# The second half of a block's first output products one step later, with a filter load and a transposed class moved

## The chip, the cores and the metric

The kernel runs on one core of a Trainium2 chip. The time is device microseconds of one execution. A core has TensorE (PE, matrix products into the banks of PSUM), VectorE (DVE), ScalarE (ACT), GpSimd (POOL) and SyncE (SP), each with its own queue of instructions that it works through in order, and 16 DMA engines that the queues share.[...]

## The reference

Two layers, on 8 sequences of 3008 tokens with 256 channels. The first multiplies each sequence's spectrum by a complex filter; the second is a feed-forward layer with a swish whose slope is given per hidden unit.

```
X = rfft(x, axis=1);  Y = X * (filt_r + 1j*filt_i);  y = irfft(Y, n=3008, axis=1)
h = y.reshape(24064, 256) @ w_in          # 256 -> 2048
g = h * sigmoid(beta * h)
out = g @ w_out                           # 2048 -> 256, float32
```

## The kernel before

The feed-forward layer is the backbone. Its 24064 tokens are 47 blocks of 512, and a block has 16 steps, one for each 128 hidden units (`fb`, 0 to 15): 752 steps. A step (the loop at L812) first makes the hidden layer, two products of 512 columns into a PSUM tile `hps` (L825), from a pool of two banks. ScalarE then makes the activation tile `gT` from it (L834; a ring of four). Then come the units that the plan has for this step. Last come the output products of the step two earlier (`LAG = 2`): four products of 256 columns, one for each 128 tokens of the block (`tb`), with `gT` as the loaded weights and a row group of `wout_sb` as the moving operand (L860). They add up over the 16 steps of a block into two accumulators `acc`, each one PSUM bank that holds two `tb`. The accumulators come from the pool `opsum`, which has three banks. After `fb` 15 each accumulator is copied to an `ost` tile and stored by SyncE. VectorE does these copies, except that ScalarE does the first of the two in the blocks 0 to 5.

The transform is done as products in stages, 3008 = 47 x 64. For sequence 0 it is done ahead of the loop, without a trip to DRAM, and its last stage is in four classes (`g`, 0 to 3), each of which makes 752 columns of the transformed sequence that the blocks then read in order. Class 0 is made before the loop. The others are units in the plan: `turn_z(g, i)` transposes (eight products on TensorE into the tile `pz`, L536, and a copy on VectorE), twice for a class, and `last_z(g, i)` makes four small products and a copy (L544), four times for a class. A block of sequence 0 can run only when its classes are there.

For the sequences 1 to 7 the stages are units in the plan. `s1` (16 for a sequence; L619) makes one product and a copy into a buffer `a1`, and each fourth one issues a store to DRAM on SyncE (L624). `a1` comes from the pool `apool` of three, in which the first class of sequence 0 also has its place. `a2_read` reads that back in four DMAs (L631). `s23` (15 for a sequence) does two products (L641), three VectorE operations with the filter tiles `frr` and `fri` (L652, L653, L656), a sum on GpSimd (L657), and three units later two more products (L667) and a copy on ScalarE. `zz_read` and `s4` (L544) give the outputs. All PSUM tiles of these units come from `fpsum`, three banks.

The plan is a table from step to units. `place(a, z, units, clear, per)` (L696) spreads units evenly over the steps a to z, in order; a step that already holds `per` units is passed over. Units run in a step in the order in which they were placed.

The tile `frr` has two uses. Ahead of the loop two thirds of it (columns 8 to 23) stage `w_out` on its way in; then it takes the real part of the filter, in three parts of 1 MB, each four DMAs of 256 KB on SyncE (`load_filter`, L127). In the kernel before, the first part is issued ahead of the loop (L520), behind a marker DMA (L506) that waits for x of sequence 1 to land. The other two parts are issued in step 15 (`uf`, L731), behind `a2_read(1)`.

Of the kernel before, what the change touches and what calls it, by code (L numbers as in the profile page):

```python
# [9 lines left out]
P = 128  # L10
# [14 lines left out]
M = 64  # L25
H = M // 2
NK = 24
J = 32
KG = 6
NG = NK // KG  # L30
JG = 8
# [6 lines left out]
def kernel(  # L38
# [10 lines left out]
    nc = tc.nc  # L49
# [8 lines left out]
    NFB = FF // P  # L58
# [29 lines left out]
    frr = consts.tile([P, NK, D], F32, name="frr", tag="frr")  # L88
# [12 lines left out]
    wout_sb = wpool.tile([P, NFB, D], BF16, name="wout_sb", tag="wout_sb")  # L101
# [25 lines left out]
    def load_filter(f_sb, filt, at, k0, n, eng):  # L127
        lo = AP(filt.tensor, filt.offset + k0 * D, [[N1 * D, H], [1, n * D]])
        hi = AP(filt.tensor, filt.offset + (N1 - k0) * D, [[N1 * D, H], [-D, n], [1, D]])
        return [  # L130
            lambda: eng.dma_start(
                f_sb[at : at + H, k0 : k0 + n, :].rearrange("p k d -> p (k d)"), lo
            ),
            lambda: eng.dma_start(f_sb[at + H : at + M, k0 : k0 + n, :], hi),
        ]
# [13 lines left out]
    def scale_wout(i):  # L149
        fs = slice(i * WG, (i + 1) * WG)  # L150
        nc.gpsimd.tensor_tensor(
            wout_sb[:, fs, :],
            staged(i),
            rbeta_sb[:, fs].unsqueeze(2).broadcast_to([P, WG, D]),
            ALU.mult,
        )
# [360 lines left out]

    for i in range(4):
        scale_wout(i)
    for at in (0, M):  # L520
        for go in load_filter(frr, filt_r, at, 0, JG, nc.sync):
            go()

    ys = {}
    ys[0] = ypool.tile([P, NDC, NK * P], BF16, name="y", tag="y")
# [4 lines left out]
    def turn_z(g, i, on_act=False):  # L530
        if g not in zz0:
            zz0[g] = zzpool.tile([KP, JG, D], BF16, name="zz", tag="zz")
        pz = fpsum.tile([P, 4, D], BF16, name="pz", tag="f")
        for e in range(4):
            for dc in range(NDC):
                nc.tensor.transpose(  # L536
                    pz[:KP, e, dc * P : (dc + 1) * P], z_t[:, dc, JG * g + 4 * i + e, :], ident[:]
                )
        evac(zz0[g][:, 4 * i : 4 * i + 4, :], pz[:KP], on_act)
# [24 lines left out]
    def last_z(g, i, on_act, own=None):  # L564
        jq, dc = divmod(i, NDC)
        c = g * JG // JC + jq
        yv = ys[0][:, dc, c * CLS : (c + 1) * CLS].rearrange("p (n j) -> p n j", j=JC)

        n0 = NP if jq == 0 else (TB - CLS) // JC
        return last4(zz0[g], t4b, JC * jq, dc, yv, on_act, own, n0)  # L570
# [55 lines left out]
    def a2_read(b):  # L626
        s = st[b]
        s["a2"] = []
        for h in range(NG):
            t = a2pool.tile([P, KG, D], BF16, name="a2", tag="a2")  # L630
            nc.sync.dma_start(t[:], s["d1c"][:, h * KG : (h + 1) * KG, :])  # L631
            s["a2"].append(t)
# [41 lines left out]
    def zz_read(b):  # L674
        s = st[b]
        s["zz"] = []
        for h in range(NJG):
            t = zzpool.tile([KP, JG, D], BF16, name="zz", tag="zz")
            nc.sync.dma_start(t[:], s["d2r"][:, h * JG : (h + 1) * JG, :])
            s["zz"].append(t)  # L680
# [15 lines left out]
    def place(a, z, units, clear=False, per=1):  # L696
        last_at = a
        for n, go in enumerate(units):
            at = a + (z - a) * n / max(1, len(units) - 1)
            at = max(int(at), last_at)  # L700
            if clear and (at % NFB < 2 or at % NFB > 13):
                at += (2 - at) % NFB
            while len(plan.get(at, ())) >= per:
                at += 1
            plan.setdefault(at, []).append(go)
            last_at = at
        return last_at

    def u1(b, act=False):
        def unit(i):  # L710
            def go():
                if i == 0:
                    start(b)
                s1(b, i, act and i % 2 == 1)

            return go

        return [unit(i) for i in range(J // 2)]

    def u23(b):  # L720
        return [lambda i=i: s23(b, i) for i in range(NK // 2 + VLAG)]

    def u4(b, act=False):
        return [lambda i=i: s4(b, i, act and i % 2 == 1) for i in range(J // 2)]

    def uz(g, act=False):
        return [lambda i=i: turn_z(g, i) for i in range(2)] + [
            lambda i=i: last_z(g, i, act) for i in range(2 * NDC)
        ]

    def uf():  # L731
        return [
            go
            for k0 in range(JG, NK, JG)
            for at in (0, M)
            for go in load_filter(frr, filt_r, at, k0, JG, nc.sync)
        ]


    def ut(n):  # L740
        return [
            lambda k=k: nc.vector.tensor_scalar_mul(
                t3[M:P, k : k + NK // n], t3b[M:P, k : k + NK // n], -1.0
            )
            for k in range(0, NK, NK // n)
        ]
# [6 lines left out]

    place(2, 14, uz(1, True))
    place(15, 29, uz(2))
    place(34, 58, uz(3, True))

    first_step = [(S * b // TB) * NFB for b in range(B + 1)]
    if B > 1:
        units = u1(1, True)  # L760
        place(3, 8, units[: J // 4], per=2)
        at = place(9, 14, units[J // 4 :], per=2)
        place(at + 1, at + 1, [lambda: a2_read(1)] + uf(), per=9)
        place(14, 20, ut(4), per=2)
        at = place(25, 56, u23(1), per=2)
        assert at < 60
        place(60, 60, [lambda: zz_read(1)], per=9)
        place(67, 79, u4(1), per=2)
    if B > 2:
        place(36, 36, ux(2), per=9)  # L770
        at = place(50, 66, u1(2, True), per=3)
        assert at < 74
        place(74, 74, [lambda: a2_read(2)], per=9)
    for b in range(2, B):
        a = first_step[b - 1]
# [36 lines left out]
    for s in range(len(steps) + LAG):  # L812
        if s < len(steps):
            i, fb = steps[s]
            t0 = i * TB
            tn = min(TB, TOK - t0)
            hps = hpsum.tile([P, TB], F32, name="hps", tag="hps")
            pos = t0
            while pos < t0 + tn:
                b, n0 = divmod(pos, S)  # L820
                ln = min(S - n0, t0 + tn - pos)
                if s == 0:
                    ln = min(ln, CLS - n0 % CLS)
                for dc in range(NDC):
                    nc.tensor.matmul(  # L825
                        hps[:, pos - t0 : pos - t0 + ln],
                        lhsT=win_sb[:, dc, fb * P : (fb + 1) * P],
                        rhs=ys[b][:, dc, n0 : n0 + ln],
                        start=(dc == 0),
                        stop=(dc == NDC - 1),  # L830
                    )
                pos += ln
            gT = gpool.tile([P, TB], BF16, name="gT", tag="gT")
            nc.scalar.activation(  # L834
                gT[:, :tn], hps[:, :tn], ACT.Silu, scale=beta_sb[:, fb : fb + 1]
            )
            blk[s] = gT
        if s in plan:
            for go in plan[s]:
                go()  # L840
        if s >= LAG:
            i, fb = steps[s - LAG]
            t0 = i * TB
            tn = min(TB, TOK - t0)
            nch = tn // P
            gT = blk.pop(s - LAG)

            last = i == NBLK - 1
            if fb == 0 and not last:
                acc = [opsum.tile([P, 2, D], F32, name="acc", tag="acc") for _ in range(2)]  # L850
            elif fb == 0:
                acc = [
                    (fpsum if h % 2 else opsum).tile(
                        [P, 1, D], F32, name="acc", tag="f" if h % 2 else "acc"
                    )
                    for h in range(nch)
                ]
            per = acc[0].shape[1]
            for tb in range(nch):
                nc.tensor.matmul(  # L860
                    acc[tb // per][:, tb % per, :],
                    lhsT=gT[:, tb * P : (tb + 1) * P],
                    rhs=wout_sb[:, fb, :],
                    start=(fb == 0 and tb % per == 0),
                    stop=(fb == NFB - 1),
                    skip_group_check=True,
                )
            if fb == NFB - 1:
                for h, a in enumerate(acc):
                    if h * per % 2 == 0:  # L870
                        ost = ostp.tile([P, 2, D], F32, name="ost", tag="ost")
                    c = h * per % 2
                    on_act = h == 0 and i < 6 or last and h % 2 == 0
                    evac(ost[:, c : c + per, :], a[:], on_act)
                    eng = nc.scalar if last and h >= 2 else nc.sync
                    store(t0 + h * per * P, per * P, ost[:, c : c + per, :], eng)
# [30 lines left out]
```

## Time and profile before

| | |
|---|---|
| median of 3 runs | 789.7 us (789.14 to 792.92) |
| profiled execution | 789.54 us |
| its span, first to last instruction | 787.6 us |
| TensorE busy | 776.5 us, 99% |
| ScalarE busy | 597.0 us, 76% |
| VectorE busy | 393.6 us, 50% |
| GpSimd busy | 144.5 us, 18% |
| granted TensorE clock | 1.000 |
| DMA | 91.46 MB, 116 GB/s on average |

A line of a group of instructions has the line of the kernel, engine, operation, output and inputs, shape and count; then the busy time in us and the mean of one in ns; then the idle time of the engine just before them and what ended most of it. A line of a timeline has start and duration in us, engine, line, operation, tiles and count, and in brackets idle time before it with its releaser. The chain is the work that ended last, followed back from the last instruction.

### The profile page before, as it was taken

What the parts mean: (1) busy time and instruction counts of PE and PEld (TensorE: products, weight loads), DVE (VectorE), ACT (ScalarE), POOL (GpSimd) and SP (SyncE); (2) the same over time, 40 slices, a digit from 0 to 9 for tenths busy, and PEclk for the clock granted to TensorE, in tenths of its full rate; (3) what the DMA queues carried; (4) which work ended last, traced back from release to release, by engine and by line L of the source; (5) the groups of instructions that cost most, each with busy time, mean ns of one, the idle gap of its engine ahead of it and who ended that gap; (6) DMA issues with size and microseconds to landing.
All of it is one profiled execution on the core that took longest, in us unless ns stands there. A gap on an engine that the chain in (4) does not pass through costs nothing.

```text
span 787.6 us, 15550 instructions
## 1 busy us (share of the span) xinstructions
PE 776.5 (99%) x6111; PEld 548.0 (70%) x6111; DVE 393.6 (50%) x645; ACT 597.0 (76%) x922; POOL 144.5 (18%) x143
## 2 busy tenths in 40 slices
PE   8999999999999999999999999999999999999998
PEld 5767667766777667876668766686667766776665
DVE  8837835646436564465635746267462761500101
ACT  6977886886678866788677876778767788677776
POOL 8512500420014200231002310024000340000000
PEclk9999999999999999999999999999999999999999
DMA  9978673517801187012850238412370214100101
GB/s 192 251 170 226 161 202 134 126 67 198 223 27 67 51 211 206 28 67 96 202 170 27 95 105 185 151 56 84 111 208 28 75 67 127 48 34 28 55 27 54
DMA packets 84185, 91.46 MB, mean 116 GB/s; under 512 B 4498, under 2 KB 74276, under 8 KB 83154
## 3 DMA queue, kind: packets, MB, share of 16 engines
q1 hardware_dynamic: 81008, 73.95, 30.5%
q0 software_dynamic: 2816, 16.26, 10.6%
q8 instruction: 48, 0.79, 0.4%
q14 instruction: 25, 0.20, 0.1%
q10 hardware_dynamic: 288, 0.26, 0.1%
HBM read 57.16 MB, written 46.66 MB: 132 GB/s over the span
## 4 chain that ended last, share of the span: by engine, by line
PE 93%; DVE 4%; issue 2%; DMA 1%; ACT 1%; DVEq 0%; ACTq 0%
PE acc L860 41%; PE hps L825 40%; PE ps L619 3%; PE ps L544 3%; PE ps L641 2%; PE ps L667 2%; PE pw L187 1%; DVE ost L109 1%; DMA d<-a 1%; DVE qb_t L444 1%; DVE pb_t L444 0%; DVE q_t L656 0%; ACT gT L834 0%; DVE q_t L653 0%; PE psa L325 0%
## 5 line engine op out<-in xcount | busy, mean ns | idle before, releaser
L834 ACT ACTIVATE gT<-hps,beta_sb 128x512 bf16<-128x512 f32 x752 | 516.2, 687 | 175.3 <-PE hps L825 164.1
L860 PE MATMUL acc<-wout_sb,gT 128*128 128x256 bf16 x3008 | 455.2, 272 | 1.2 <-ACT ost L107 0.2
L825 PE MATMUL hps<-y,win_sb 128*128 128x512 bf16 (+8 forms) x1730 | 447.7, 351 | 0.3 <-ACT gT L834 0.3
L860 PEld LDWEIGHTS <-gT 128*128 128x128 bf16 x3008 | 285.4, 98 | 132.4 <-issue 4.3
L825 PEld LDWEIGHTS <-win_sb 128*128 128x128 bf16 x1730 | 164.9, 98 | 24.8 <-issue 0.6
L657 POOL TENSOR_TENSOR v_t<-p_t,q_t 128x512 bf16<-128x512 f32 x84 | 106.7, 1271 | 393.1 <-DVE q_t L656 390.2
L109 DVE COPY ost<-acc 128x512 f32<-128x512 f32 (+1 forms) x88 | 56.3, 678 | 193.8 <-PE acc L860 190.6
L109 DVE CAST a<-ps 96x512 bf16<-96x512 f32 x96 | 65.8, 686 | 90.0 <-PE ps L619 85.3
L111 DVE TENSOR_SCALAR y<-ps 128x376 bf16<-128x376 f32 (+1 forms) x119 | 64.5, 545 | 62.6 <-PE ps L544 62.4
L652 DVE TENSOR_TENSOR p_t<-ps,frr 128x512 f32<-128x512 f32 x84 | 58.1, 692 | 32.0 <-PE ps L641 27.9
L656 DVE TENSOR_TENSOR q_t<-ps,fri 64x512 f32<-64x512 f32 x84 | 58.3, 694 | 1.2
L653 DVE SCALAR_TENSOR_TENSOR q_t<-ps,fri 64x512 f32<-64x512 f32 x84 | 57.4, 684 | 1.1
L544 PEld LDWEIGHTS <-zz 96*128 96x128 bf16 x512 | 35.3, 97 | 30.6 <-issue 1.9
L107 ACT ACTIVATE z<-ps 128x512 bf16<-128x512 f32 x84 | 49.5, 590 | 1.0 <-PE ps L667 0.9
L619 PE MATMUL ps<-xg,t 94*96 94x512 bf16 x112 | 42.0, 381 | 0.0
L544 PE MATMUL ps<-t,zz 96*128 96x94 bf16 x448 | 36.7, 204 | 0.0
L667 PE MATMUL ps<-v_t,t 128*128 128x256 bf16 x168 | 32.1, 273 | 0.8 <-DVE q_t L656 0.8
L641 PE MATMUL ps<-a,t 128*128 128x256 bf16 x168 | 32.1, 273 | 0.0
L118 POOL DMA_DIRECT2D xg<-in_x_dram x22 | 12.1, 552 | 101.7 <-PE acc L860 97.7
L641 PEld LDWEIGHTS <-t 128*128 128x128 bf16 x168 | 15.8, 98 | 14.6
L619 PEld LDWEIGHTS <-t 94*96 94x96 bf16 x112 | 13.8, 123 | 12.1
L667 PEld LDWEIGHTS <-t 128*128 128x128 bf16 x168 | 15.4, 98 | 8.5 <-DVE q_t L656 1.5
(120 smaller groups left out, 196.3 us busy)
## 6 DMA issues: line engine op xcount, KB each, us to landing
out_dram<-ost SPq DMA_DIRECT2D x80, 256.0 KB, 2.1
d<-a SPq DMA_DIRECT2D x28, 384.0 KB, 3.8
a<-d SPq DMA_DIRECT2D x28, 384.0 KB, 4.9
d<-z SPq DMA_DIRECT2D x28, 384.0 KB, 2.3
zz<-d SPq DMA_DIRECT2D x28, 384.0 KB, 6.7
xg<-in_x_dram POOLq DMA_DIRECT2D x6, 1280.0 KB, 10.1
frr<-in_filt_r_dram SPq DMA_DIRECT2D x12, 256.0 KB, 7.7
out_dram<-ost SPq DMA_DIRECT2D x18, 128.0 KB, 2.1
```

Source lines behind the costliest of these rows:

```text
L109: nc.vector.tensor_copy(dst, src)
L111: nc.vector.tensor_scalar_mul(dst, src, scale)
L544: nc.tensor.matmul(ps[:, e, :NP], lhsT=zz[:, jj + e, dc * P : (dc + 1) * P], rhs=tab[:], start=True, stop=True,)
L619: nc.tensor.matmul(ps[:KP], lhsT=t1[:], rhs=s["x"][:, 2 * i : 2 * i + 2, :], start=True, stop=True)
L641: nc.tensor.matmul(ps[:, e, :], lhsT=t2[:, k0 + e, 3:5, :].rearrange("p c k -> p (c k)"), rhs=s["a2"][g][:, kk + e, :], start=True, stop=True,
L652: nc.vector.tensor_tensor(p_t[:], ps[:], frr[:, ks_, :], ALU.mult)
L656: nc.vector.tensor_tensor(q_t[:M], ps[M:P], fri[M:P, ks_, :], ALU.mult)
L657: nc.gpsimd.tensor_tensor(v_t[:], p_t[:], q_t[:], ALU.add)
L667: nc.tensor.matmul(ps[:, e, :], lhsT=t3[:, k0 + e, :], rhs=v_t[:, e, :], start=True, stop=True)
L825: nc.tensor.matmul(hps[:, pos - t0 : pos - t0 + ln], lhsT=win_sb[:, dc, fb * P : (fb + 1) * P], rhs=ys[b][:, dc, n0 : n0 + ln], start=(dc ...
L834: nc.scalar.activation(gT[:, :tn], hps[:, :tn], ACT.Silu, scale=beta_sb[:, fb : fb + 1])
L860: nc.tensor.matmul(acc[tb // per][:, tb % per, :], lhsT=gT[:, tb * P : (tb + 1) * P], rhs=wout_sb[:, fb, :], start=(fb == 0 and tb % per = ...
```

## The change

There are three edits.

In the loop, the output products of `fb` 0 are cut in two. The step makes those of the first accumulator only. Those of the second are made in the following step, between the two pairs of `fb` 1.

The first third of the filter load is taken from ahead of the loop and put in the plan at step 10, ahead of that step's other units. `uf` gets bounds for it. For the first stage of sequence 1 the limit of units in a step is raised from 2 to 9, so that the entry at step 10 pushes none of them away.

The units of class 3 of sequence 0 are placed in two pieces: the two `turn_z` at the steps 20 to 24, and the four `last_z` spread over 34 to 58. Before, the six were spread over 34 to 58.

```
-    for at in (0, M):
-        for go in load_filter(frr, filt_r, at, 0, JG, nc.sync):
-            go()
...
-    def uf():
+    def uf(a, z):
         return [
             go
-            for k0 in range(JG, NK, JG)
+            for k0 in range(a, z, JG)
             for at in (0, M)
             for go in load_filter(frr, filt_r, at, k0, JG, nc.sync)
         ]
...
-    place(34, 58, uz(3, True))
+    units = uz(3, True)
+    place(20, 24, units[:2], per=2)
+    place(34, 58, units[2:])
...
-        at = place(9, 14, units[J // 4 :], per=2)
-        place(at + 1, at + 1, [lambda: a2_read(1)] + uf(), per=9)
+        place(10, 10, uf(0, JG), per=9)
+        at = place(9, 14, units[J // 4 :], per=9)
+        place(at + 1, at + 1, [lambda: a2_read(1)] + uf(JG, NK), per=9)
...
-            for tb in range(nch):
+            todo = [(gT, fb, tb) for tb in range(nch)]
+            if fb == 0:
+                todo, late = todo[: nch // 2], todo[nch // 2 :]
+            elif fb == 1:
+                todo[nch // 2 : nch // 2] = late
+            for g_, f_, tb in todo:
                 nc.tensor.matmul(
                     acc[tb // per][:, tb % per, :],
-                    lhsT=gT[:, tb * P : (tb + 1) * P],
-                    rhs=wout_sb[:, fb, :],
-                    start=(fb == 0 and tb % per == 0),
-                    stop=(fb == NFB - 1),
+                    lhsT=g_[:, tb * P : (tb + 1) * P],
+                    rhs=wout_sb[:, f_, :],
+                    start=(f_ == 0 and tb % per == 0),
+                    stop=(f_ == NFB - 1),
                     skip_group_check=True,
                 )
```

By the plan the units move so:

| unit | step before | step after |
|---|---|---|
| `turn_z(3, 0)`, `turn_z(3, 1)` | 34, 38 | 20, 24 |
| `last_z(3, 0)` to `last_z(3, 3)` | 43, 48, 53, 58 | 34, 42, 50, 58 |
| `s1(1, 9)`, `s1(1, 12)` | 10, 12 | 9, 11 |
| first third of the filter | ahead of the loop | 10 |
| one of four VectorE units that negate a table (L742) | 20 | 21 |

## The prediction

> **What bounds the kernel now.** I read the page first, then the order of time on TensorE, then the engines that its gaps name.
>
> ```profile
> span 787.6 us, 15550 instructions
> PE 776.5 (99%) x6111; PEld 548.0 (70%) x6111; DVE 393.6 (50%) x645; ACT 597.0 (76%) x922; POOL 144.5 (18%) x143
> PE 93%; DVE 4%; issue 2%; DMA 1%; ACT 1%; DVEq 0%; ACTq 0%
> L860 PE MATMUL acc<-wout_sb,gT 128*128 128x256 bf16 x3008 | 455.2, 272 | 1.2 <-ACT ost L107 0.2
> ```
>
> TensorE is the bound: 99% busy, 93% of the chain. The page counts only 11 us of idle time on it, but a matmul's end is modelled, so a short wait hides inside "busy". I therefore take start-to-start times. Two 512-column products take 0.43 us, four 256-column ones 0.44 (109 ns each). The timeline of TensorE at the edge between blocks 7 and 8:
>
> ```profile
> 177.38 0.60 PE L860 MATMUL acc<-wout_sb,gT 128*128 128x256 bf16 x4
> 177.82 0.59 PE L825 MATMUL hps<-y,win_sb 128*128 128x512 bf16 x2
> 178.25 0.38 PE L667 MATMUL ps<-v_t,t 128*128 128x256 bf16 x2
> 178.47 0.83 PE L860 MATMUL acc<-wout_sb,gT 128*128 128x256 bf16 x4
> 179.13 0.59 PE L825 MATMUL hps<-y,win_sb 128*128 128x512 bf16 x2
> ```
>
> From 178.47 to 179.13 are 0.66 us where 0.44 are work: the third of four products started 0.23 us late. VectorE's timeline says why:
>
> ```profile
> 177.58 0.69 DVE L109 CAST a<-ps 96x512 bf16<-96x512 f32 x1 [0.40 <-PE ps L619]
> 178.19 1.27 DVE L109 COPY ost<-acc 128x512 f32<-128x512 f32 x2
> ```
>
> The pool of accumulators has three banks and a block takes two, so the second accumulator of block 8 is the first of block 7, which VectorE empties until about 178.85. I read the same pair of starts at all 46 edges; the wait is there at 31, always between the second and third product. Blocks 3 to 5: 0.15, 0.18, 0.40 us, together 0.73. Then every six blocks (two sequences) the same four: 0.23, 0.28, 0.14, 0.08, together 0.73, five times, 3.65. Blocks 39 to 46: 0.14 and seven of 0.08, 0.69. **Sum 5.07 us.**
>
> In the first 100 us there are larger gaps. TensorE, SyncE's queue and VectorE at the first:
>
> ```profile
> 52.26 0.59 PE L825 MATMUL hps<-y,win_sb 128*128 128x512 bf16 x2
> 54.43 0.33 PE L544 MATMUL ps<-t4b,zz 96*128 96x94 bf16 x4 [1.58 <-ACT a L107]
> ```
>
> ```profile
> 45.26 0.23 SPq L506 DMA_DIRECT2D mark<-xg  x1
> 45.53 0.31 SPq L131 DMA_DIRECT2D frr<-in_filt_r_dram  x1
> 45.88 0.42 SPq L134 DMA_DIRECT2D frr<-in_filt_r_dram  x1
> 46.35 0.45 SPq L131 DMA_DIRECT2D frr<-in_filt_r_dram  x1
> 46.84 0.42 SPq L134 DMA_DIRECT2D frr<-in_filt_r_dram  x1
> 47.37 9.34 SPq L624 DMA_DIRECT2D d<-a  x4
> ```
>
> ```profile
> 53.80 1.28 DVE L109 CAST a<-ps 96x512 bf16<-96x512 f32 x2 [4.75 <-DMA d<-a]
> ```
>
> SyncE is held at the marker until x of sequence 1 has landed (45.24), then issues the first third of the filter (1 MB), then the first store of stage 1. That store lands at 53.68 by its semaphore, and the fourth stage-1 buffer is the one it frees. VectorE and ScalarE wait for it, and TensorE, out of PSUM slots, starts 1.74 us late. Later VectorE is the slow one while it does the filter products of sequence 1 (66 to 91 us without a pause), and TensorE waits for PSUM slots:
>
> ```profile
> 75.71 0.61 PE L536 MATMUL pz<-ident,z_t 128*96 128x128 bf16 x8 [0.27 <-DVE q_t L656]
> 81.43 0.39 PE L667 MATMUL ps<-v_t,t 128*128 128x256 bf16 x2 [0.54 <-DVE q_t L656]
> 88.53 0.39 PE L667 MATMUL ps<-v_t,t 128*128 128x256 bf16 x2 [0.24 <-DVE q_t L656]
> ```
>
> By starts these are 0.43, 0.71 and 0.40 us late.
>
> **What the Trainium skill says.** "TensorE: Matmul & The Clock Gate", section "Wait — 56ns, not 53.3ns?": warm matmuls start N ÷ 2.4 GHz plus about 2.5 ns apart. The trace agrees (256 columns: 106.7 + 2.3 ns), so what exceeds this is waiting. "PSUM — Partial Sum Buffer", section "Engine vs sequencer instructions": matmuls start and complete in program order; so the hidden layer's products wait behind a late third product, as at 179.13. "DMA: Bandwidth & Descriptors", section "Issuing engines are not separate DMA queues": all queues share 16 engines; with its section "Two DMAs through the same engine are not ordered" (descriptors of a queue start in order), the store behind 1 MB is no surprise. The trace: issue to landing 6.3 us there, 3.1 us for the fourth store, issued alone at 56.41.
>
> **The change, part by part.**
>
> *Late half.* No instruction is added. At fb 0 two products remain; their partners run one step later, between the two pairs of fb 1. The second accumulator's first write now follows 0.22 us after the step's first product. It goes behind the next hidden products (0.43) and the next first pair (0.22), so 0.65 us later than now, more where the step has planned work. The longest wait is 0.40, so all 31 should vanish: −5.07. Behind the new place stand three products of the same step and the next hidden products; if the bank were late there, they would wait just as now. The fb 0 activation is kept a step longer: ring of four, next writer at step +4, whose hidden products come after the late pair in TensorE's order, so no wait. The shortened step lets the next hidden products ask 0.22 us earlier for their PSUM bank, freed by ScalarE. In a step without planned work a bank is free again 0.59 + 0.11 + 0.69 + 0.06 = 1.45 us after its products start (product, start of the activation, activation, release) and asked for after 2 × 0.87 − 0.22 = 1.52. That is hidden by 0.07 us. If this cover is gone, it costs at most 0.22 at each edge. I take 0; ends −5.1 and, with half of it lost, −2.5.
>
> *Filter reload.* Four DMAs of 256 KB, issue 1.6 us together, go past two stage-1 stores on SyncE's queue, to step 10. The first store is issued at about 45.5 and, at the 3.1 us of an undisturbed one, lands near 48.6; its buffer is asked for at about 49.5 and TensorE needs it only near 51.6. So −1.74. The reload then issues near 47.5 to 49.5 and moves 1 MB in 4 to 5 us (before: 46 to 51), landing near 54. The third store queues behind it; the fourth is issued near 54.4 and lands near 57.5 (before 59.47). All four gate the readback of stage 1, whose first part took about 5 us: near 63, for a first use at 64.8. The filter's first use is the same. Both hidden. With cover gone the cost is the lateness itself.
>
> *Two stage-1 products* (ninth and twelfth, counted from 0) go one step earlier because the limit of a step was raised: same work, ScalarE and VectorE have gaps there: 0 to +0.2, taken 0.
>
> *Turned class.* Sixteen transposes (2 × 0.45 us of TensorE) go from steps 34 and 38 to 20 and 24; their two evacuations on VectorE (0.71 us each by the next start) leave the crowded stretch for one where VectorE has waits. The four last products with them go from 43, 48, 53, 58 to 34, 42, 50, 58. Between step 25 and step 50 TensorE has 0.9 less to do, VectorE 1.4; before step 25 TensorE has 0.9 more. If VectorE binds all through, the net is −0.5. By the PSUM slots of the built program, step 34 still waits for the same product of VectorE (0.43 stays), step 38's 0.71 goes, and step 42 may wait 0.2 in place of 0.40: −0.9. But x of sequence 2 is next: it landed at 94.22 and was first used at 95.09. Its load stands on GpSimd's queue behind the sixth filter sum, which comes 1.7 us sooner (0.84 from the start of the stretch, 0.71 from one evacuation, the rest a pause of VectorE), while step 50 comes about 2.5 us sooner. The 0.87 us of cover is then about used up. I take −0.6; ends −1.5 and +0.5.
>
> Sum: −5.07 − 1.74 − 0.6 = −7.4. The profiled execution took 789.54 (span 787.6 and 1.9 around it): 782.1. The median of the runs is 0.16 above it, so **782.3**, rounded up to 782.4 for small losses.
>
> **Rivals.**
> - *Front eaten.* x of sequence 2, or the readback behind the reload, arrives late and takes back the 2.3 us of the front; the edges are untouched. For: 0.87 us of cover on x, shared DMA engines. Against: both loads also start earlier. 789.7 − 5.07 − 0.3 = 784.3.
> - *Edges move to ScalarE.* The wait for the hidden layer's bank takes the place of the wait for the accumulator. For: a margin of 0.07 us. Against: edges with planned work have 0.2 more. Half of 5.07 left, and the front's 1.74 with nothing from the turned class: 785.4; if all is lost, 787.4. I put it at 786.4.
> - *Slower.* The reload at step 10 stands ahead of the third and fourth store and so of the readback; if the readback's first part comes L us after 64.8, TensorE stops for L, since every slot then holds a filter product. Nothing is gained from L = 7.4 on; with L = 11, 793. Against: 11 us would be some 2.5 MB more in front, and the reload is 1 MB.
> - *It does nothing.* The late half still waits at its new place: excluded unless VectorE is over 0.65 us behind, which no edge shows.
>
> **How the numbers follow.** All parts as worked out: 0.70 (782.4). Front eaten: 0.18 (784.3). Edges move: 0.08 (786.4). Slower: 0.04. A difference of 0.5% (3.95 us, about what a measurement of this kernel can tell) ends at 785.75: faster 0.70 + 0.18 = 0.88, same 0.08, slower 0.04. The likeliest case alone spans 781.2 (all of 5.07, 1.74 and 1.5 gained) to 783.6; the range reaches to the second: 781.0 to 785.3.
>
> **What will show it.** Between the second and third accumulator product of fb 0, now in different steps, no late start at any edge; runs of two and of six products at each edge. No wait of ScalarE or VectorE for the store of stage 1 near 50 us. The two evacuations of the turned class before 66 us and less waiting at TensorE's third-stage products near 80. Wrong if hidden products start late just after an edge (ScalarE), or stage-1 products of sequence 2 late near 92 us (x), or the first filter products late near 64 us (readback).

## The result and the profile after

| | changed kernel | kernel before |
|---|---|---|
| median of the runs | 785.83 us (785.11 to 786.2, 6 runs) | 789.24 us (787.54 to 792.92, 6 runs) |
| profiled execution | 785.37 us | 789.54 us |
| its span | 783.3 us | 787.6 us |

The changed kernel is faster, by a ratio of 0.9952 [0.9933, 0.9971]: 3.4 us by the medians of the table, 3.8 by the ratio. The forecast was a gain of 7.4 and a time of 782.4, with a range of 781.0 to 785.3. The time lies just above the range, and about half of the gain is missing.

The page of the changed kernel, the lines that answer to those shown of before:

```profile
span 783.3 us, 15454 instructions
PE 768.8 (98%) x6015; PEld 547.8 (70%) x6111; DVE 393.3 (50%) x645; ACT 594.4 (76%) x922; POOL 144.4 (18%) x143
PE 96%; ACT 1%; issue 1%; DMA 1%; DVE 1%; POOL 0%; DVEq 0%; POOLq 0%
L867 PE MATMUL acc<-wout_sb,gT 128*128 128x256 bf16 x3008 | 451.4, 272 | 2.7
```

TensorE is the bound as before. VectorE's share of the chain fell from 4% to 1%. The counts also say how far the busy time can be trusted: 6111 weight loads but 6015 matmuls. 96 matmuls have no record in this trace, so busy time and idle time between records are both a little wrong, and I go by starts again.

TensorE's timeline at the edge between the blocks 7 and 8, where the kernel before lost 0.23 us:

```profile
175.38 0.60 PE L867 MATMUL acc<-wout_sb,gT 128*128 128x256 bf16 x4
175.81 0.60 PE L825 MATMUL hps<-y,win_sb 128*128 128x512 bf16 x2
176.25 0.38 PE L664 MATMUL ps<-v_t,t 128*128 128x256 bf16 x2
176.46 0.38 PE L867 MATMUL acc<-wout_sb,gT 128*128 128x256 bf16 x2
176.68 0.59 PE L825 MATMUL hps<-y,win_sb 128*128 128x512 bf16 x2
177.11 0.38 PE L616 MATMUL ps<-xg,t 94*96 94x512 bf16 x1
177.33 0.82 PE L867 MATMUL acc<-wout_sb,gT 128*128 128x256 bf16 x6
```

Two output products, the next hidden products, then six output products: 0.22 and 0.65 us to the next start, no gap. None of the 46 edges has a late accumulator product any more; a second profile of this kernel ("The changed kernel again", below), which has all 6111 matmul records, shows the same. The edge loss of 5.07 us is gone whole.

The first gap of the front is gone too. SyncE's timeline, and TensorE's at the place where it had been 1.74 us late:

```profile
44.58 0.23 SPq L506 DMA_DIRECT2D mark<-xg  x1
44.92 2.71 SPq L621 DMA_DIRECT2D d<-a  x2
47.68 0.53 SPq L131 DMA_DIRECT2D frr<-in_filt_r_dram  x1
```

```profile
52.73 0.59 PE L825 MATMUL hps<-y,win_sb 128*128 128x512 bf16 x2
53.16 0.33 PE L541 MATMUL ps<-t4b,zz 96*128 96x94 bf16 x4
```

0.43 us from one to the other is work alone. The stores now stand ahead of the filter load. Each of the four stores landed 3.1 us after its issue. Later in the front two of the three waits for VectorE remain, and the one of 0.71 us is gone:

```profile
75.34 0.33 PE L541 MATMUL ps<-t4b,zz 96*128 96x94 bf16 x4 [0.48 <-DVE q_t L653]
84.58 0.39 PE L664 MATMUL ps<-v_t,t 128*128 128x256 bf16 x2 [0.26 <-DVE q_t L653]
```

By starts they are 0.43 us each (a missing record stands in the first of these gaps). So far all is as forecast. A small new wait stands at the edge into block 3, at the filter unit of its `fb` 3:

```profile
93.68 0.59 PE L825 MATMUL hps<-y,win_sb 128*128 128x512 bf16 x2
94.40 0.39 PE L664 MATMUL ps<-v_t,t 128*128 128x256 bf16 x2
```

```profile
93.65 0.69 DVE L653 TENSOR_TENSOR q_t<-ps,fri 64x512 f32<-64x512 f32 x1
```

L664 was due at 94.11 and started at 94.40, 0.29 us late, after the end of a filter operation of VectorE at 94.34. The view of waits names this operation as what released the product's weight load.

The larger loss shows in the same view, one line of which grew. It gives the waiting engine and line, the releaser, then the idle time in us, the count and the longest one. Before:

```profile
PEld L667 <- ACT z L107: 0.3, 1, 0.3
```

After:

```profile
PEld L664 <- ACT z L107: 3.8, 12, 0.5
PE ps L664 <- ACT z L107: 0.2, 1, 0.2
```

(L667 before and L664 after are the same product, the third stage in `s23`; L107 is the copy on ScalarE that empties its PSUM tile.) The 3.8 us are idle time of the weight load, ordinary pauses included. By the starts of the products the loss is smaller, as follows. TensorE and ScalarE of the changed kernel at one of the twelve places, the edge into block 7:

```profile
160.19 0.38 PE L664 MATMUL ps<-v_t,t 128*128 128x256 bf16 x2
160.41 0.38 PE L867 MATMUL acc<-wout_sb,gT 128*128 128x256 bf16 x2
160.62 0.59 PE L825 MATMUL hps<-y,win_sb 128*128 128x512 bf16 x2
161.06 0.38 PE L638 MATMUL ps<-a,t 128*128 128x256 bf16 x2
161.46 0.39 PE L664 MATMUL ps<-v_t,t 128*128 128x256 bf16 x2
161.69 0.82 PE L867 MATMUL acc<-wout_sb,gT 128*128 128x256 bf16 x6
```

```profile
160.23 0.69 ACT L834 ACTIVATE gT<-hps,beta_sb 128x512 bf16<-128x512 f32 x1 [0.18 <-PE hps L825]
160.81 0.59 ACT L107 ACTIVATE z<-ps 128x512 bf16<-128x512 f32 x1
```

Two units of `s23` stand in the consecutive steps `fb` 2 and 3. (Their products share a turn of TensorE's order with the output products of `fb` 0 and 1, which come two steps late; that is why the short step falls just between them.) The two L638 products at 161.06 take 0.22 us, so L664 was due at 161.28 and started at 161.46, about 0.19 us late. The copy of the previous unit ended at 160.81 + 0.59 = 161.40; 0.06 us later the product starts. In the built program, both products have the same bank of `fpsum`, and the view of waits names this copy as the releaser.

The kernel before at the same place:

```profile
162.38 0.38 PE L667 MATMUL ps<-v_t,t 128*128 128x256 bf16 x2
162.60 0.60 PE L860 MATMUL acc<-wout_sb,gT 128*128 128x256 bf16 x4
163.04 0.59 PE L825 MATMUL hps<-y,win_sb 128*128 128x512 bf16 x2
163.47 0.38 PE L641 MATMUL ps<-a,t 128*128 128x256 bf16 x2
163.69 0.38 PE L667 MATMUL ps<-v_t,t 128*128 128x256 bf16 x2
```

```profile
163.01 0.59 ACT L107 ACTIVATE z<-ps 128x512 bf16<-128x512 f32 x1
```

The copy ended at 163.60 and the product started when it was due, at 163.69. From one L664 (L667) product to the next the bank needs 1.27 us, as the changed kernel shows (160.19 to 161.46: 0.62 to the start of the copy, 0.59 of copy, 0.06 to the product). The kernel before gave it 1.31. The late half takes two output products, 0.22 us, out of exactly this stretch, and leaves 1.09.

So the theory after the result: **the late half takes 0.22 us of cover from a bank that ScalarE's copy holds between two filter units in consecutive steps.** The places are twelve: blocks 6 and 7, 12 and 13, and so on to 36 and 37. By starts, eleven of them are 0.187 or 0.188 us late, where they were not late before. At block 6 a wait of 0.168 became 0.383. Together 11 × 0.1875 + 0.215 = 2.28 us. It comes from the way the plan keeps the units of sequences 2 to 7 clear of the edges (`clear`, in `place`): a unit that falls on `fb` 14, 15, 0 or 1 goes to `fb` 2, or to 3 if 2 is taken.

The rivals: the front lost something that the profile doesn't show as a wait, or the edges lost it at the bank of the hidden layer, as the forecast's rival had it.

### The profile page after: what moved, and what is told of

It is laid out like the page before. It is cut to its first block, busy times and chain, and to the rows that moved or that the text cites. A ratio compares the mean times of both kernels' runs of the same rounds, so it can differ in the third digit from the quotient of the medians.

```text
span 783.3 us, 15454 instructions
## 1 busy us (share of the span) xinstructions
PE 768.8 (98%) x6015; PEld 547.8 (70%) x6111; DVE 393.3 (50%) x645; ACT 594.4 (76%) x922; POOL 144.4 (18%) x143
## 4 chain that ended last, share of the span: by engine, by line
PE 96%; ACT 1%; issue 1%; DMA 1%; DVE 1%; POOL 0%; DVEq 0%; POOLq 0%
PE acc L867 43%; PE hps L825 39%; PE ps L616 3%; PE ps L541 3%; PE ps L664 3%; PE ps L638 2%; DMA xg<-in_x_dram 1%; PE psz L461 1%; PE pz L533 0%; PE psa L325 0%; ACT a L107 0%; DVE q_t L653 0%; DVE q_t L650 0%; PE pt L351 0%; PE ps L435 0%
## 5 line engine op out<-in xcount | busy, mean ns | idle before, releaser
L825 PE MATMUL hps<-y,win_sb 128*128 128x512 bf16 (+8 forms) x1636 | 427.6, 350 | 0.4 <-ACT gT L834 0.3
L107 ACT ACTIVATE z<-ps 128x512 bf16<-128x512 f32 x84 | 49.5, 589 | 0.0
L664 PE MATMUL ps<-v_t,t 128*128 128x256 bf16 x168 | 32.2, 274 | 0.8 <-DVE q_t L653 0.3
L638 PE MATMUL ps<-a,t 128*128 128x256 bf16 x168 | 32.1, 273 | 0.4
L638 PEld LDWEIGHTS <-t 128*128 128x128 bf16 x168 | 15.8, 98 | 14.6
L664 PEld LDWEIGHTS <-t 128*128 128x128 bf16 x168 | 15.3, 98 | 10.8 <-ACT z L107 3.8
```

Source lines behind the costliest of these rows:

```text
L638: nc.tensor.matmul(ps[:, e, :], lhsT=t2[:, k0 + e, 3:5, :].rearrange("p c k -> p (c k)"), rhs=s["a2"][g][:, kk + e, :], start=True, stop=True,
L664: nc.tensor.matmul(ps[:, e, :], lhsT=t3[:, k0 + e, :], rhs=v_t[:, e, :], start=True, stop=True)
L825: nc.tensor.matmul(hps[:, pos - t0 : pos - t0 + ln], lhsT=win_sb[:, dc, fb * P : (fb + 1) * P], rhs=ys[b][:, dc, n0 : n0 + ln], start=(dc ...
```

## The experiments

The runs were made in three sets, each beside the kernel before on the same chip: its median was 789.66 for the first four, 789.63 for the next four, 789.55 for the last.

### The loop edit alone

The kernel before with the edit of the loop only; plan and filter load stay as they were.

```
-            for tb in range(nch):
+            todo = [(gT, fb, tb) for tb in range(nch)]
+            if fb == 0:
+                todo, late = todo[: nch // 2], todo[nch // 2 :]
+            elif fb == 1:
+                todo[nch // 2 : nch // 2] = late
+            for g_, f_, tb in todo:
...
```

> The kernel before with the late half alone. Theory (third-stage bank): the 31 waits at the edges go (-5.07 us); in their place the third-stage products of the filter unit at fb 3 wait about 0.19 us for the PSUM bank that ScalarE's z copy of the unit at fb 2 still holds, at the blocks 6, 7, 12, 13 ... 36, 37 (12 places, 2.3 us), because the shortened step took 0.22 us of cover from between them. Net -2.7 us, 786.5; nothing changes before step 50. Rival (the front failed, the edges paid in full): -5.1 us, 784.2, no wait at those 12 places. Rival (hidden layer's bank behind ScalarE): late hidden products just after plain edges, 0.1 to 0.2 us at each of 46.

786.82 us, ratio 0.9966 [0.9954, 0.9979]: 2.8 us faster. All edges are clean in its trace, and the front has its old waits. The new wait is there whole:

```profile
PEld L667 <- ACT z L107: 3.8, 12, 0.5
```

By starts it is 0.385 once and 0.188 eleven times. 5.07 less 2.28 is 2.8, what the medians give. Counted from one activation of ScalarE to the next, its trace gains 2.41 us from step 50 on; the 0.4 between the two is taken up under "Why the prediction was wrong". Its edge into block 3 gains nothing: a product of stage 1 is 0.17 us late there, behind VectorE. The late half makes the loss by itself.

### The front alone

The changed kernel with the old loop over `tb`:

```
-            todo = [(gT, fb, tb) for tb in range(nch)]
...
-            for g_, f_, tb in todo:
+            for tb in range(nch):
...
```

> The changed kernel with the output products of fb 0 whole again: the moved filter reload and the moved class alone. Theory (third-stage bank): the front keeps its gain, 1.7 to 1.9 us at step 14 and 0.6 to 0.9 up to step 50, so -2.4 us, 786.8; the waits at the edges are as before (5.1 us) and none at the 12 third-stage places. Rival (front eaten later): under 0.5 us faster than before.

787.15 us, ratio 0.9970 [0.9959, 0.9982]: 2.5 us faster. The waits at the edges are back, at 30 places with 4.9 us; the one at block 3 (0.15 us before) has shrunk to 0.02, and the filter unit behind it is 0.02 us late, not 0.29. Of the twelve new waits only the one at block 6 is there, 0.165 us as before. ScalarE's activation of step 50 starts at 93.06, against 95.51 before. Counted from the first activation that is 2.43 us sooner, and nothing takes it back: the last one comes 2.54 sooner. The forecast was 2.34, and the rival "front eaten" falls. The two halves sum to 5.1 us by their ratios, 5.4 by the medians.

### The filter units one step further from the edge

The bound in `place`, on top of the changed kernel. No filter unit of the sequences 2 to 7 stands at `fb` 2 any more, in the edge's short step, and two consecutive ones, now at `fb` 3 and 4, have the step of six products between them:

```
-            if clear and (at % NFB < 2 or at % NFB > 13):
-                at += (2 - at) % NFB
+            if clear and (at % NFB < 3 or at % NFB > 13):
+                at += (3 - at) % NFB
```

> The changed kernel, where filter units that are kept clear of an edge start at fb 3 and not at fb 2, so that the two units on consecutive steps have the step of six products between them and not the step of two. Theory (third-stage bank): the 12 waits of 0.19 us go, about 2.4 us faster than the changed kernel, 783.4. Rival (hidden layer's bank, or a loss elsewhere): within 0.5 us of the changed kernel, 785.8.

782.47 us, ratio 0.9910 [0.9896, 0.9924]. The view of waits has no line of L664 behind the copy. TensorE and ScalarE at the same edge:

```profile
159.29 0.59 PE L825 MATMUL hps<-y,win_sb 128*128 128x512 bf16 x2
159.72 0.38 PE L638 MATMUL ps<-a,t 128*128 128x256 bf16 x2
159.94 0.38 PE L664 MATMUL ps<-v_t,t 128*128 128x256 bf16 x2
160.16 0.82 PE L867 MATMUL acc<-wout_sb,gT 128*128 128x256 bf16 x6
160.81 0.59 PE L825 MATMUL hps<-y,win_sb 128*128 128x512 bf16 x2
161.25 0.38 PE L638 MATMUL ps<-a,t 128*128 128x256 bf16 x2
161.46 0.38 PE L664 MATMUL ps<-v_t,t 128*128 128x256 bf16 x2
```

```profile
160.57 0.59 ACT L107 ACTIVATE z<-ps 128x512 bf16<-128x512 f32 x1
```

Now the long step of six output products lies between the two units: 159.94 to 161.46, 1.52 us, and the copy is done at 161.16. This kernel beats the kernel before and the changed one, and its time is what the forecast had for the change, 782.4. It does not by itself show that the bank was the whole cause, since it moves many units; hence the next.

### The late half left out at the twelve places

The plan is that of the changed kernel. Blocks 6, 7, 12, 13 to 36, 37 keep the old order:

```
-            if fb == 0:
+            if fb == 0 and 6 <= i < 38 and i % 6 < 2:
+                late = []
+            elif fb == 0:
```

> The changed kernel without the late half at the 12 blocks 6, 7, 12, 13 ... 36, 37, whose edges had no accumulator wait before; the plan is untouched. Theory (third-stage bank): the 12 waits go and none of the old ones comes back, so as fast as with the units at fb 3, about 783.4 to 783.6. Rival (loss elsewhere): 785.8, as the changed kernel.

782.88 us, ratio 0.9914 [0.9900, 0.9928]. One of the twelve waits is left, the 0.165 us at block 6:

```profile
PEld L664 <- ACT z L107: 0.3, 1, 0.3
```

The gain comes back with no unit moved.

### Three products late instead of two

On the changed kernel, so that the short step is 0.109 us shorter still (one product):

```
-                todo, late = todo[: nch // 2], todo[nch // 2 :]
+                todo, late = todo[:1], todo[1:]
             elif fb == 1:
-                todo[nch // 2 : nch // 2] = late
+                todo[1:1] = late
```

> The changed kernel with three of the four products of fb 0 moved to the next step, not two: the step is shorter by another 0.109 us. Theory (cover between two third-stage products): each of the 12 waits grows from 0.19 to 0.30 us, +1.3 us on the changed kernel; and the hidden layer's bank, asked for 1.41 us after it was last taken where 1.45 are needed, begins to show at edges without planned work, 0.04 us at some 10 to 46 places, +0.4 to +1.9. Together 1.7 to 3.2 us slower than the changed kernel. Rival (the waits come from elsewhere): the 12 waits stay 0.19 us.

786.58 us, ratio 0.9966 [0.9953, 0.9979]; 1.7 us more than the changed kernel in the same set (784.89, below). TensorE and ScalarE at the edge into block 7:

```profile
161.75 0.38 PE L638 MATMUL ps<-a,t 128*128 128x256 bf16 x2
162.26 0.39 PE L664 MATMUL ps<-v_t,t 128*128 128x256 bf16 x2
```

```profile
161.62 0.59 ACT L107 ACTIVATE z<-ps 128x512 bf16<-128x512 f32 x1
```

The second starts 0.51 us behind the first where 0.22 is work. Over the places the lateness by starts is 0.298 us eleven times and 0.496 once: the step got 0.109 shorter, each wait 0.110 longer. That is a cover that is used up, on which each nanosecond counts in full. In this kernel the hidden layer's bank shows for the first time: at 13 edges the hidden products start 0.019 to 0.024 us late, about 0.27 in all. Eleven times 0.110, 0.113 at block 6 and these 0.27 make 1.6 of the 1.7 us. The margin of 0.07 us that the forecast gave for that bank was about right: 0.109 less the 0.02 of lateness is 0.09.

### The moved units on the kernel before

The control: the same edit as in the third experiment, on the kernel before, without the late half.

```
-            if clear and (at % NFB < 2 or at % NFB > 13):
-                at += (2 - at) % NFB
+            if clear and (at % NFB < 3 or at % NFB > 13):
+                at += (3 - at) % NFB
```

> The kernel before, with nothing but the filter units kept clear to fb 3. Theory: there is no shortened step, so the third-stage products had their bank in time anyway; the same as before within 0.5 us (one wait of 0.17 us at 147 us may go). Rival (the later units are a gain by themselves): faster by 2 us or more, as at the step from the changed kernel to units at fb 3.

791.13 us, ratio 1.0022 [1.0012, 1.0032]. I had expected no change, and missed: 1.5 us slower by the medians, 1.7 by the ratio. (Its profiled execution took 789.60, one of the fastest of its 22, 789.32 to 795.30: it is one without the gap at step 14. From step 60 on it falls behind the profile of before by 1.38 us.) The starts at the edges say why. Waits of the accumulator are now at 44 edges, 6.39 us together, in place of 31 with 5.07. TensorE at the edge into block 7:

```profile
161.09 0.68 PE L860 MATMUL acc<-wout_sb,gT 128*128 128x256 bf16 x4
161.60 0.59 PE L825 MATMUL hps<-y,win_sb 128*128 128x512 bf16 x2
```

0.51 us where 0.44 are work; the kernel before had 162.60 to 163.04 at this edge, none late. There a filter unit at `fb` 2, with 0.43 us of products, ran in front of these four and hid the copy of the accumulator. Thirteen edges lost such cover: 0.40 us at block 6 and 0.08 at twelve. Against these 1.32 us, the filter unit's wait of 0.17 at block 6 is gone. So the third experiment's edit by itself is a loss. The late half takes away the wait for the accumulator, and only with that gone is the place of the unit free to choose.

### The filter reload alone

On the kernel before; the load ahead of the loop goes, and `uf` gets its bounds as in the change:

```
...
-        at = place(9, 14, units[J // 4 :], per=2)
-        place(at + 1, at + 1, [lambda: a2_read(1)] + uf(), per=9)
+        place(10, 10, uf(0, JG), per=9)
+        at = place(9, 14, units[J // 4 :], per=9)
+        place(at + 1, at + 1, [lambda: a2_read(1)] + uf(JG, NK), per=9)
```

> The kernel before with the filter reload at step 10 (and the two stage-1 products a step earlier) alone. Theory: the wait at step 14 goes (1.74 us in the profile of before, 0.76 in that of the late half alone), the waits for VectorE from 75 to 90 us stay (1.5 us): 0.8 to 1.8 us faster than before. Rival (the reload delays the readback): the first filter products at step 25 start late, no gain.

788.09 us, ratio 0.9978 [0.9969, 0.9988]: 1.5 us faster by the medians, 1.7 by the ratio. The gap at step 14 is gone; the later waits of 0.43, 0.56 and 0.40 us are there. (The middle one is 0.71 in the first profile of the kernel before, 0.56 here and in the run with the loop edit alone.)

### The turned class alone

On the kernel before:

```
-    place(34, 58, uz(3, True))
+    units = uz(3, True)
+    place(20, 24, units[:2], per=2)
+    place(34, 58, units[2:])
```

> The kernel before with the moved class alone. Theory: of the waits for VectorE between 75 and 90 us (0.43, 0.71, 0.40) the 0.71 goes, and one of 0.43 and one of 0.2 to 0.4 stay; 0.6 to 0.9 us faster than before, and with the reload's 1.7 this gives the 2.4 of both. The wait at step 14 stays where an execution has it (0 to 1.7 us in the profiles so far). Rival (the transposes only change place): within 0.3 us of before.

788.53 us, ratio 0.9991 [0.9982, 1.0000]: about 1.0 us by the medians, 0.7 by the ratio. The interval reaches 1, so the times alone hardly show a gain; in the trace the middle wait is gone and two stay, and from step 14 to step 50 it takes 0.69 us less than the kernel before. By the ratios the reload and the class give 1.7 and 0.7 us, together 2.4, what the front alone gave. Within these intervals, of 0.7 to 0.8 us to each side, nothing shows that the two touch each other.

### The changed kernel again

> The changed kernel itself, on the chip of these runs. Theory: the late half gains 2.7 and the front 2.4 us, so 0.9935 of before, and 2.3 us slower than the kernel with units at fb 3. Rival (a loss not yet found, which the first comparison's 3.4 us would need): 0.9955.

784.89 us, ratio 0.9942 [0.9930, 0.9954]: 4.7 us faster. This time lies inside the forecast's range, where the first (785.83) lay just above it; the two intervals overlap. The theory's 0.9935 is inside this interval and the rival's 0.9955 just outside. The profile agrees, with the new waits of 0.387 us once and 0.188 eleven times. The third experiment's kernel, which has none of them, is at 782.47, 2.4 us less, for a sum of 2.28 by starts.

## Why the prediction was wrong, and where it was right

**Edges: right.** The 31 waits for the accumulator went whole, 5.07 us, with the runs of two and of six products as described, and no accumulator is late at the new place.

**The step that failed** is in "Late half", the sentence on the shortened step: it lets TensorE ask for banks 0.22 us earlier, "hidden by 0.07 us", and "I take 0; ends −5.1 and −2.5". That step looked at three things which a shorter step meets: the accumulator, the ring of `gT` and the hidden layer's bank. It left out the fourth, the bank of `fpsum`, at those places where two filter units stand in consecutive steps, and so put this loss at nothing. There the cover was 0.04 us by the period (1.31 given, 1.27 needed). The short step takes 0.22, and what the cover doesn't hide is waited for: 0.188 us at eleven places and 0.215 more than before at one, 2.28 us by starts, shown by two runs that take it away in different ways (782.47 and 782.88) and by one that makes it longer (0.110 us of wait for 0.109 of step). With this term in the sum, 789.54 − 5.07 + 2.28 − 2.34 = 784.4. The changed kernel's medians are 785.83 and 784.89.

Where the rest went can be read from the starts of ScalarE's activations, one for each step, in the profile of before and the two of the changed kernel:

| stretch | gain in the sum | gain in the two profiles |
|---|---|---|
| up to the first activation | 0 | −0.48, −0.03 |
| from there to step 50 | 2.34 | 2.43, 2.42 |
| step 50 to 60, the edge into block 3 | 0.15 | −0.11, −0.11 |
| step 60 to the last | 2.64 | 2.42, 2.40 |

The first row is scatter of what lies ahead of the loop: the first activation starts between 36.4 and 37.5 us in the profiles, with no order by edit. The third row is the same oversight at a thirteenth place. There the product waits for VectorE and not for ScalarE: 0.29 and 0.17 us in the changed kernel's profiles, 0.02 with the front alone, where the step is not shortened. (With the loop edit alone it is the product of stage 1 behind it that waits, 0.17 us.) The front alone gains 0.11 in this stretch, so the late half loses there the 0.22 that it took out of the step. The last row is a matter of counting. From step to step each of the twelve waits costs 0.196 us and not 0.188, since the second product of the pair is late by a further 0.011, and an edge gives back about 0.005 us less than the sum has for it. The last two rows are also the 0.4 us by which the trace of the loop edit alone gains less than 2.8.

The rival "edges move to ScalarE" named the right engine and nearly the right size, 786.4, but the wrong bank; the size came from halving a sum and not from a count of places, so its nearness is luck. (Its other figure, 787.4, does not follow from its terms: 789.7 less the front's 1.74 is 788.0; 787.4 has the turned class's 0.6 in it too.) The hidden layer's bank never was late in the changed kernel. Its argument against itself, that edges with planned work have 0.2 us more, was the very error: planned work gives the hidden layer's bank cover, but brings a bank of its own, which ScalarE reaches only after the activation. The sign to watch for ("hidden products start late just after an edge") would therefore not have found it; the line of L664 behind the copy in the waits does.

**Filter reload: right.** 1.7 us forecast, 1.5 by the medians and 1.7 by the ratio of the run with the reload alone. Readback and first filter products were not late. The forecast had one profile's wait as if it were fixed, though, on which more below.

**Turned class: right in the mechanism.** 0.6 forecast, 0.7 by the ratio (its interval runs from 0 to 1.4) and 0.69 in the trace, largely by the waits that were named: 0.43 stays and 0.71 goes. The last one, for which 0.2 was forecast in place of 0.40, stayed at 0.43. The cover of x for sequence 2 was used up, as the forecast feared, but at little cost: in the changed kernel's first profile it landed at 93.08, and the product that uses it started at 93.24, 0.01 us late. In the six other profiles with the moved class this product was 0.03 to 0.12 us late, 0.14 after the landing.

**Range and chances.** The low end of the working for the edges, −2.5, was the nearest to what came (−2.8), but the forecast gave that case 8 in 100, since it was tied to the one bank that had been checked. This end was half of the whole as well, and its agreement is luck.

## What to carry to other kernels

On a saturated engine that works in order, products moved out of a step are cover taken from every wait that spans this step: list all banks that are written on both sides of it, planned work included, and compare the period each is given with what it needs (product, copy, and whatever stands ahead of the copy on its engine), place by place. The Trainium skill, "Perfetto Trace Analysis", section "Optimization Strategy", says that a gap which repeats on the engine that should be saturated can mean too little SBUF or PSUM for the next tile; both repeating waits of this case were PSUM banks (0.08 to 0.40 us at the edges before, 0.19 at the filter units after). And a unit that looks free to move may be what hides another wait, as the control showed: make the moves in the order in which they free each other.

## What was not expected of the hardware

The gap at step 14 of the kernel before is not a fixed amount. It follows the moment at which x of sequence 1 has landed and the marker DMA goes: marker at 43.66, 44.31, 45.26 and 45.62 us, gap 0, 0.76, 1.74 and 1.97 us, in four profiles of kernels with the old order of that queue. SyncE's line of the control, the one without the gap:

```profile
43.66 0.23 SPq L506 DMA_DIRECT2D mark<-xg  x1
```

From its first activation to step 60 this execution takes 1.88 us less than the profile of before, as does the profile with the reload alone: the reload gains what an execution loses at this gap.

That the forecast's 1.74 agreed with the effect over the runs (1.5 by the medians, 1.7 by the ratio) is partly luck: a loss read from a single profile that hangs on when a DMA lands should get a range from the scatter of that landing.
